# Six heads' masks in one transfer of 128 rows, and three pairs' k transposed on TensorE

## The chip, the core and the metric

One NeuronCore of a Trainium2 chip runs the whole kernel. The metric is the device time of one execution in microseconds (us), less is better; the median of several runs is compared. The profiles show one execution each.

## What is computed

Three stages follow each other. The change touches the first one only.

```python
q, k, v: (2, 8, 768, 64) float32;  lam: (8,), 0.97 to 0.99
# attention with decay, in blocks of 64 positions
Dmask = where(i >= j, lam[h] ** (i - j), 0)
out   = (q @ k.T * Dmask) @ v + (q * lam[h] ** (i + 1)) @ kv_state
kv_state = lam[h] ** block * kv_state + (k * lam[h] ** (block - 1 - j)).T @ v
# x = out as (2, 768, 512); then a token mixer and a channel MLP
h  = relu(x^T @ w_tok1) @ w_tok2;     u  = x + h^T
y  = u + relu(u @ w_ch1) @ w_ch2
# then real(fft2(y)), a norm and a second MLP (512 -> 2048 -> 512), each with a residual
```

## The kernel before, in words

**Tiling of the attention.** The kernel takes blocks of C = 128 positions (NC = 6 a sequence), which gives the same result as blocks of 64. Two heads share the 128 partitions; such a *pair* is the unit. There are NP = 4 pairs for each of 2 batches, numbered 0 to 7 (pairs 4 to 7 are the second batch). Positions within a block are stored in reverse for k, v and kT, so that a mask entry depends on the sum of row and column.

**What a pair loads.** `load_kp` reads k with head dimensions on the partitions (kT, 384 KB) into one of four places `kps` of the tile `kp`; place i serves pairs i and i + 4. `load_qkv` reads q (same layout), and k and v with positions on the partitions, into a tile `qkv_b_hp` of three used quarters of 384 KB each; its last quarter takes `qs`, q times the powers of lam. k thus comes from memory twice, in two layouts.

**What a pair computes.** `attention_scores` (s): 24 matmuls of kT with q into PSUM; VectorE multiplies them with the masks `dT` (line 420) into `st`; GpSimd makes `qs` (line 424). `attention_states` (u): ScalarE scales k by the decay (line 438, in place), TensorE multiplies it with v into a bank `u_...`, and VectorE runs the chain of states (lines 448 and 450). `attention_out` (r): ScalarE puts the states into block diagonals (line 462), TensorE adds `st` times v and the state times `qs` in banks `po_...`, and ScalarE copies them to `xT` (line 473).

**The masks.** `dT` holds one 128 x 128 mask for each of 8 heads, in the tile `att`. Those of heads 0 and 1 are built on VectorE by doubling (line 374). For the other six, the powers of lam are built in `pw8`, one partition a head (line 341), written to a scratch in memory (line 344), and read back by `skew` (line 350) so that partition p gets the row that starts at p: first heads 2 to 5, then 6 and 7, in pieces of 512 bytes.

**What sets the order.** TensorE and SP, which issues the loads, run in program order as the code writes it; the other engines' order is placed by a scheduler at build time. The string `EARLY` is the program of the first 90 us: `s`, `u`, `r` with a pair's number, `l` loads a pair (4 to 7), `c` and `d` convert token weights (a weight arrives as 64-bit words and takes one copy on ScalarE, two or three shifts on VectorE and a split on ScalarE and GpSimd), `w` is 8 transposes of the identity that only keep TensorE busy, `x`, `h`, `o` are the token mixer. 22 further such transposes (`keep_warm(22)`) stand ahead of it. At most eight loads are under way at once: each issue waits for the landing of the eighth before it. The tile pools are rings: PSUM banks of `acc_bank` (4) serve `u`, `po`, the warm-up and x; `half_tile` (5) holds the pairs' qkv tiles and later x.

Of the kernel before, what the change touches and what calls it, by code (L numbers as in the profile page):

```python
# [11 lines left out]
F32 = mybir.dt.float32  # L12
# [3 lines left out]
AF = mybir.ActivationFunctionType  # L16
# [19 lines left out]

EARLY = """s0 w u0 w s1 r0 u1 s2 u2 l4 r1 s3 u3 c r2 s4 l5 r3 u4 d d d x00 s5 l6 u5 r4 s6 x01 h00 c r5 c h01 l7 u6 s7 u7 r6 o00
r7 m o01 x10 m x11 m h10 m h11 m m o10 o11 k"""
# [24 lines left out]
def body(ctx: ExitStack, tc: tile.TileContext, qkv, kT, lam, w_tok1, w_tok2,  # L63
# [154 lines left out]
    def stage_abs():  # L218

        if at_["abs"] >= at_["load"]:  # L220
            return
        job = jobs[at_["abs"]]
        kind, key = job
        at_["abs"] += 1
        if kind in ("single", "sums"):
            return
        m = raw_p.tile([P, 512], U32, tag="man", name="m_" + "_".join(map(str, key)), bufs=BUFS["man"])[:, :width(key)]
        mans[job] = m
        with tc.issue_after(lag.get("act", on_act["keys", 3])), behind_urgent():
            lo, hi = words(job)  # L230
            nc.scalar.activation(f32(m), f32(hi), AF.Copy, scale=DOWN)
            if key[0] in "ab":
                halves = raws[job].bitcast(U16)[:, :4 * width(key)].rearrange("p (n t) -> p n t", t=4)
                nc.scalar.activation(lo, halves[:, :, 1], AF.Identity, scale=2.0 ** -13, bias=floor_by)
# [88 lines left out]
    def attention_setup():  # L323

        pw8 = temp(2 * C, "pw8")[:H]
        nc.sync.dma_start(pw8[:, C:C + 1], lam.rearrange("(h o) -> h o", o=1))
        lam_bc = sm_p.tile([P, H], F32, name="lam_bc")
        nc.scalar.dma_start(lam_bc, lam.rearrange("(o h) -> o h", o=1).broadcast_to([P, H]))
        kp = big_tile("kp").rearrange("p (i s) -> p i s", i=4)[:, :, :S]
        kps = [kp[:, i, :].rearrange("p (c j) -> p c j", j=C) for i in range(4)]  # L330
        load_kp(0, 0, kps[0])
        t = half_tile([P, 4, S], "qkv_0_0")
        for i in range(3):
            nc.sync.dma_start(t[:, i, :], qkv[0, 0, :, i])
        load_kp(0, 1, kps[1])
        nc.vector.memset(pw8[:, 0:C - 1], 0.0)
        nc.vector.memset(pw8[:, C - 1:C], 1.0)
        n = 1
        while n < C:
            w = min(n, C - n)  # L340
            ts(out=pw8[:, C + n:C + n + w], in0=pw8[:, C:C + w], scalar1=pw8[:, C + n - 1:C + n], scalar2=None,
               op0=ALU.mult)
            n *= 2
        nc.sync.dma_start(scratch, pw8)
        att = big_tile("att")
        dT = att[:, 0:H * C].rearrange("p (h j) -> p h j", h=H)

        def skew(h0, h1):
            src = bass.AP(scratch.tensor, scratch.offset + h0 * 2 * C, [[1, P], [2 * C, h1 - h0], [1, C]])
            nc.sync.dma_start(dT[:, h0:h1, :], src)  # L350

        load_qkv(0, 1)
        skew(2, 6)

# [9 lines left out]
        while n < C:  # L364
# [7 lines left out]
            for h in range(2):  # L372
                src = bands[i % 2][:, h]
                built = stt(out=dT[:, h, :] if 2 * n == C else bands[1 - i % 2][:, h, C // 2:],
                            in0=src[:, C // 2 - n:C // 2 - n + C], scalar=by[:, h:h + 1], in1=src[:, C // 2:],
                            op0=ALU.mult, op1=ALU.add).ins
# [14 lines left out]
        pair[0, 0] = t  # L391
        return dT, pw, kps, [bd[:, i] for i in range(2)], skew

    def load_qkv(b, hp):
        t = half_tile([P, 4, S], f"qkv_{b}_{hp}")
        nc.sync.dma_start(t[:, 0, :], qkv[b, hp, :, 0])
        nc.sync.dma_start(t[:, 1:3, :], qkv[b, hp, :, 1:3])
        pair[b, hp] = t

    def load_kp(b, hp, kp):  # L400
        nc.sync.dma_start(kp, kT[b, hp].rearrange("p (c j) -> p c j", j=C))

    pair = {}

    def attention_scores(b, hp, dT, pw, kp):
# [5 lines left out]
        for g, cs in enumerate((range(4), range(4, NC))):  # L411
# [6 lines left out]
            for a in range(2):  # L418
                st = st2[:, a] if g else temp(4 * C, f"st_{n}_{a}").rearrange("p (c j) -> p c j", c=4)
                tt(out=st, in0=ps[a][:, :m * C].rearrange("p (c j) -> p c j", c=m),  # L420
                   in1=dT[:, 2 * hp + a:2 * hp + a + 1, :].to_broadcast([P, m, C]), op=ALU.mult)
                for i, c in enumerate(cs):
# [6 lines left out]
    def attention_states(b, hp, dT, pw):  # L429
# [6 lines left out]
        with tc.issue_after(on_act[behind]):  # L436
            for a in range(2):
                on_act["keys", NP * b + hp] = nc.scalar.activation(
                    kn[:, :NC - 1, a * D:(a + 1) * D], kn[:, :NC - 1, a * D:(a + 1) * D], AF.Copy,
                    scale=dT[:, 2 * hp + a, C - 1:C]).ins  # L440
        ups = acc_bank(f"u_{n}")
# [577 lines left out]
    with tc.manual_schedule(engines={ENG.SP, ENG.PE}):  # L1019
        dT, pw, kps, bds, skew = attention_setup()  # L1020

# [4 lines left out]
        load(2)  # L1026
        skew(6, H)
        load(3)
# [5 lines left out]
        def scores(n):  # L1034
            attention_scores(n // NP, n % NP, dT, pw, kps[n % NP])

        def states(n):
# [12 lines left out]
        def constants():  # L1050
# [4 lines left out]
        keep_warm(22)  # L1055
        acts = {"s": scores, "u": states, "r": result, "l": load, "c": convert, "x": token_in, "h": token_hidden,
                "o": token_out, "m": run, "w": lambda: keep_warm(8), "k": constants, "d": lambda: convert(1, load=False)}
# [148 lines left out]
```

## Time and profile before

| | |
|---|---|
| median of 3 runs | 605.16 us (603.69 to 605.57) |
| the profiled execution | 605.05 us, of which its span 603.1 |
| TensorE busy (PE) | 585.0 us, 97% of the span |
| VectorE busy (DVE) | 410.4 us, 68% |
| ScalarE (ACT), GpSimd (POOL) | 269.9 us, 45%; 138.8 us, 23% |
| granted clock of TensorE | 1.000 (full speed) over the span |
| bytes moved by DMA | 65.58 MB, mean 109 GB/s |

Busy shares are means over stages of very different kind; the attention takes the first 70 us or so, in which the token mixer already begins. A group of instructions is named by its line; `out<-in` are the program's tiles. "[x <-E]" behind a row is idle time ahead of it and what ended it.

### The profile page before, as it was taken

To read this page: it belongs to the slowest core of one execution; us is meant where nothing else is said; L and a number is where in the kernel's file an instruction comes from. 1 tells how busy PE (TensorE), PEld (TensorE's weight loads), DVE (VectorE), ACT (ScalarE), POOL (GpSimd) and SP (SyncE) were. 2 spreads that over 40 slices of the span, in tenths; PEclk is the share of its full clock that TensorE was granted. 3 is DMA by queue.
4 is the path that set the end of the run, shared out by engine and by line. 5 is a ranking of instruction groups with operands and counts; after the bars stand their busy time and mean duration, and the time that the engine had idled before them with its cause. 6 is when DMAs were issued, how large, how long until landed. Compare 5 with 4: busy or idle time off the path is not lost. (4 is left out here: it accounts for less than half of the span.)

```text
span 603.1 us, 9588 instructions
## 1 busy us (share of the span) xinstructions
PE 585.0 (97%) x3704; PEld 545.9 (91%) x3704; DVE 410.4 (68%) x768; ACT 269.9 (45%) x536; POOL 138.8 (23%) x119
## 2 busy tenths in 40 slices
PE   8789999999999999999999999999999999999997
PEld 7777899999999999999989899899899888999886
DVE  6788893474586656848796896768775765664435
ACT  2756981255475555534454451324533434431110
POOL 5252331023230041101364110013501213120000
PEclk9999999999999999999999999999999999999999
DMA  7964431014448767410232000002521232200005
GB/s 275 407 261 158 185 122 60 0 71 141 137 148 265 245 192 219 146 64 2 57 101 71 19 2 35 18 1 58 168 88 36 88 122 88 87 2 1 0 1 209
DMA packets 24637, 65.58 MB, mean 109 GB/s; under 512 B 2824, under 2 KB 3984, under 8 KB 24592
## 3 DMA queue, kind: packets, MB, share of 16 engines
q1 hardware_dynamic: 24304, 64.83, 32.1%
q8 instruction: 29, 0.48, 0.3%
q10 hardware_dynamic: 288, 0.14, 0.1%
q14 instruction: 16, 0.13, 0.1%
HBM read 54.99 MB, written 9.97 MB: 108 GB/s over the span
## 5 line engine op out<-in xcount | busy, mean ns | idle before, releaser
L526 DVE SCALAR_TENSOR_TENSOR hid<-ph,hid 128x384 fp32r<-128x384 f32 x68 | 37.6, 553 | 59.6 <-ACT hid L525 59.4
L145 PE MATMUL ac<-w_b,hid 128*128 128x512 f32 x192 | 75.8, 395 | 0.0
L144 PE MATMUL ac<-w_b,hid 128*128 128x512 f32 x192 | 75.7, 394 | 0.0
L143 PE MATMUL ac<-w_b,hid 128*128 128x512 f32 x192 | 74.9, 390 | 0.0
L143 PE MATMUL ph<-uh,w_a 128*128 128x384 f32 x192 | 64.7, 337 | 0.0
L143 PE MATMUL ac<-hid,w_b 128*128 128x384 f32 x192 | 64.5, 336 | 0.0
L144 PE MATMUL ac<-hid,w_b 128*128 128x384 f32 x192 | 64.3, 335 | 0.0
L145 PE MATMUL ph<-uh,w_a 128*128 128x384 f32 x192 | 64.2, 335 | 0.0
L145 PE MATMUL ac<-hid,w_b 128*128 128x384 f32 x192 | 64.2, 334 | 0.0
L144 PE MATMUL ph<-uh,w_a 128*128 128x384 f32 x192 | 64.2, 334 | 0.0
L525 ACT ACTIVATE hid<-ph 128x384 fp32r<-128x384 f32 x68 | 33.1, 487 | 69.3 <-PE ph L145 68.9
L287 POOL TENSOR_TENSOR w_a<-m_a,w_a 128x512 fp32r<-128x512 f32 x18 | 25.5, 1418 | 131.9 <-ACT w_a L286 131.9
L145 PEld LDWEIGHTS ac<-w_b,hid 128*128 128x128 f32 x192 | 36.0, 188 | 7.7
L144 PEld LDWEIGHTS ac<-w_b,hid 128*128 128x128 f32 x192 | 36.0, 188 | 6.1
L143 PEld LDWEIGHTS ac<-w_b,hid 128*128 128x128 f32 x192 | 36.1, 188 | 5.8
L287 POOL TENSOR_TENSOR w_b<-m_b,w_b 128x512 fp32r<-128x512 f32 x18 | 25.3, 1403 | 49.6 <-ACT w_b L286 32.4
L143 PEld LDWEIGHTS ph<-uh,w_a 128*128 128x128 f32 x192 | 36.1, 188 | 0.4 <-issue 0.2
L144 PEld LDWEIGHTS ac<-hid,w_b 128*128 128x128 f32 x192 | 36.1, 188 | 0.3 <-DVE hid L526 0.3
L144 PEld LDWEIGHTS ph<-uh,w_a 128*128 128x128 f32 x192 | 36.1, 188 | 0.1
L143 PEld LDWEIGHTS ac<-hid,w_b 128*128 128x128 f32 x192 | 36.1, 188 | 0.0
L145 PEld LDWEIGHTS ph<-uh,w_a 128*128 128x128 f32 x192 | 36.0, 188 | 0.0
L145 PEld LDWEIGHTS ac<-hid,w_b 128*128 128x128 f32 x192 | 36.0, 188 | 0.0
(504 smaller groups left out, 1467.0 us busy)
## 6 DMA issues: line engine op xcount, KB each, us to landing
qkv<-qkv SPq DMA_DIRECT2D x7, 768.0 KB, 10.0
single_scratch<-m_a SPq DMA_DIRECT2D x16, 256.0 KB, 4.4
qkv<-qkv SPq DMA_DIRECT2D x10, 384.0 KB, 5.9
kp<-kT SPq DMA_DIRECT2D x8, 384.0 KB, 6.9
out<-u SPq DMA_DIRECT2D x11, 256.0 KB, 2.1
single_scratch<-m_b SPq DMA_DIRECT2D x10, 256.0 KB, 5.3
raw_t_0d<-w_tok SPq DMA_DIRECT2D x2, 384.0 KB, 9.3
raw_t_1d<-w_tok SPq DMA_DIRECT2D x2, 384.0 KB, 2.9
```

The costliest lines, as they stand in the source:

```text
L143: nc.tensor.matmul(ps, wt[0], xt[0], start=first, stop=False, **kw)
L144: nc.tensor.matmul(ps, wt[0], xt[1], start=False, stop=False, **kw)
L145: nc.tensor.matmul(ps, wt[1], xt[0], start=False, stop=last, **kw)
L287: nc.gpsimd.tensor_tensor(out=t[:, 1, :n], in0=src, in1=f32(t[:, 0, :n]), op=ALU.subtract)
L525: mark("act", nc.scalar.activation(hi, ps, AF.Relu))
L526: mark("dve", stt(out=lo, in0=ps, scalar=0.0, in1=f32(hi), op0=ALU.max, op1=ALU.subtract))
```

## The change

The six far heads' powers are now built on one partition with the head as the inner index, so that the scratch holds x0h0, x0h1, ... One transfer (`far_masks`) fills `att` for all six: partition p reads 768 consecutive values (3 KB) that start at 6p. A head's mask is then a view of that tile in which neighbours lie six values apart (`far[:, :, h]`); heads 0 and 1 stay packed. The powers' place is that of pairs 2 and 3 in `kp`, which isn't loaded any more.

For pairs 1, 2 and 3 kT isn't read. The new `attention_turn` (word `t`) has TensorE transpose k's six blocks into two banks `pk` of the `acc_bank` ring, before k is scaled in place, and ScalarE copies them to `kps`. Loads of these pairs come one quarter at a time, k first. `t3` stands ahead of `u2`; one conversion `d` stands ahead of `u4`. Pairs 4 to 7 load kT as before.

```diff
--- before.py
+++ after.py
@@ -34,7 +34,10 @@
 BIG = 12 * NQ
 
 
-EARLY = """s0 w u0 w s1 r0 u1 s2 u2 l4 r1 s3 u3 c r2 s4 l5 r3 u4 d d d x00 s5 l6 u5 r4 s6 x01 h00 c r5 c h01 l7 u6 s7 u7 r6 o00
+TURNED = (1, 2, 3)
+
+
+EARLY = """s0 w u0 t1 w s1 r0 t2 u1 s2 t3 u2 l4 r1 s3 u3 c r2 s4 l5 r3 d u4 d d x00 s5 l6 u5 r4 s6 x01 h00 c r5 c h01 l7 u6 s7 u7 r6 o00
 r7 m o01 x10 m x11 m h10 m h11 m m o10 o11 k"""
@@ -226,7 +229,7 @@
             return
         m = raw_p.tile([P, 512], U32, tag="man", name="m_" + "_".join(map(str, key)), bufs=BUFS["man"])[:, :width(key)]
         mans[job] = m
-        with tc.issue_after(lag.get("act", on_act["keys", 3])), behind_urgent():
+        with tc.issue_after(lag.get("act", on_act[("keys", 3) if key == ("t1", 0) else ("out", 2)])), behind_urgent():
             lo, hi = words(job)
             nc.scalar.activation(f32(m), f32(hi), AF.Copy, scale=DOWN)
             if key[0] in "ab":
@@ -322,35 +325,38 @@
 
     def attention_setup():
 
-        pw8 = temp(2 * C, "pw8")[:H]
-        nc.sync.dma_start(pw8[:, C:C + 1], lam.rearrange("(h o) -> h o", o=1))
+        kp = big_tile("kp").rearrange("p (i s) -> p i s", i=4)[:, :, :S]
+        kps = [kp[:, i, :].rearrange("p (c j) -> p c j", j=C) for i in range(4)]
+
+
+        n_far = H - 2
+        powers = kp[0:1, 2:4, :].rearrange("o i s -> o (i s)").rearrange("o (x h) -> o x h", h=n_far)
+        nc.sync.dma_start(powers[:, C:C + 1, :], lam[2:H].rearrange("(o x h) -> o x h", o=1, x=1))
         lam_bc = sm_p.tile([P, H], F32, name="lam_bc")
         nc.scalar.dma_start(lam_bc, lam.rearrange("(o h) -> o h", o=1).broadcast_to([P, H]))
-        kp = big_tile("kp").rearrange("p (i s) -> p i s", i=4)[:, :, :S]
-        kps = [kp[:, i, :].rearrange("p (c j) -> p c j", j=C) for i in range(4)]
         load_kp(0, 0, kps[0])
         t = half_tile([P, 4, S], "qkv_0_0")
-        for i in range(3):
-            nc.sync.dma_start(t[:, i, :], qkv[0, 0, :, i])
-        load_kp(0, 1, kps[1])
-        nc.vector.memset(pw8[:, 0:C - 1], 0.0)
-        nc.vector.memset(pw8[:, C - 1:C], 1.0)
+        nc.sync.dma_start(t[:, 0, :], qkv[0, 0, :, 0])
+        nc.vector.memset(powers[:, 0:C - 1, :], 0.0)
+        nc.vector.memset(powers[:, C - 1:C, :], 1.0)
         n = 1
         while n < C:
             w = min(n, C - n)
-            ts(out=pw8[:, C + n:C + n + w], in0=pw8[:, C:C + w], scalar1=pw8[:, C + n - 1:C + n], scalar2=None,
-               op0=ALU.mult)
+            tt(out=powers[:, C + n:C + n + w, :], in0=powers[:, C:C + w, :],
+               in1=powers[:, C + n - 1:C + n, :].to_broadcast([1, w, n_far]), op=ALU.mult)
             n *= 2
-        nc.sync.dma_start(scratch, pw8)
+        nc.sync.dma_start(scratch.rearrange("(o n) -> o n", o=1), powers.rearrange("o x h -> o (x h)"))
+        for i in range(1, 3):
+            nc.sync.dma_start(t[:, i, :], qkv[0, 0, :, i])
         att = big_tile("att")
-        dT = att[:, 0:H * C].rearrange("p (h j) -> p h j", h=H)
-
-        def skew(h0, h1):
-            src = bass.AP(scratch.tensor, scratch.offset + h0 * 2 * C, [[1, P], [2 * C, h1 - h0], [1, C]])
-            nc.sync.dma_start(dT[:, h0:h1, :], src)
-
-        load_qkv(0, 1)
-        skew(2, 6)
+        far = att[:, 2 * C:H * C].rearrange("p (j h) -> p j h", h=n_far)
+        dT = [att[:, h * C:(h + 1) * C] for h in range(2)] + [far[:, :, h] for h in range(n_far)]
+
+        def far_masks():
+            nc.sync.dma_start(att[:, 2 * C:H * C], bass.AP(scratch.tensor, scratch.offset, [[n_far, P], [1, n_far * C]]))
+
+        load_kp(0, 1, kps[1])
+        load_qkv(0, 1, far_masks)
 
         bands = [temp(2 * (C // 2 + C), f"band_{i}").rearrange("p (h j) -> p h j", h=2) for i in range(2)]
         for t_ in bands:
...
@@ -389,16 +395,32 @@
                                     in1=pw[:, :, n - 1:n].to_broadcast([P, NP, n]), op=ALU.mult)
             n *= 2
         pair[0, 0] = t
-        return dT, pw, kps, [bd[:, i] for i in range(2)], skew
-
-    def load_qkv(b, hp):
+        return dT, pw, kps, [bd[:, i] for i in range(2)]
+
+    def load_qkv(b, hp, first=lambda: None):
         t = half_tile([P, 4, S], f"qkv_{b}_{hp}")
-        nc.sync.dma_start(t[:, 0, :], qkv[b, hp, :, 0])
-        nc.sync.dma_start(t[:, 1:3, :], qkv[b, hp, :, 1:3])
+        if NP * b + hp in TURNED:
+            nc.sync.dma_start(t[:, 1, :], qkv[b, hp, :, 1])
+            first()
+            for i in (2, 0):
+                nc.sync.dma_start(t[:, i, :], qkv[b, hp, :, i])
+        else:
+            nc.sync.dma_start(t[:, 0, :], qkv[b, hp, :, 0])
+            nc.sync.dma_start(t[:, 1:3, :], qkv[b, hp, :, 1:3])
         pair[b, hp] = t
 
     def load_kp(b, hp, kp):
-        nc.sync.dma_start(kp, kT[b, hp].rearrange("p (c j) -> p c j", j=C))
+        if NP * b + hp not in TURNED:
+            nc.sync.dma_start(kp, kT[b, hp].rearrange("p (c j) -> p c j", j=C))
+
+    def attention_turn(b, hp, kp):
+        kn = pair[b, hp][:, 1, :].rearrange("p (c j) -> p c j", j=C)
+        for g, cs in enumerate((slice(0, 4), slice(4, NC))):
+            m = len(range(NC)[cs])
+            pk = acc_bank(f"pk_{b}_{hp}_{g}")
+            for i in range(m):
+                nc.tensor.transpose(pk[:, i * C:(i + 1) * C], kn[:, cs.start + i, :], ident)
+            nc.scalar.activation(kp[:, cs, :], pk[:, :m * C].rearrange("p (c j) -> p c j", c=m), AF.Copy)
 
     pair = {}
 
@@ -418,7 +440,7 @@
             for a in range(2):
                 st = st2[:, a] if g else temp(4 * C, f"st_{n}_{a}").rearrange("p (c j) -> p c j", c=4)
                 tt(out=st, in0=ps[a][:, :m * C].rearrange("p (c j) -> p c j", c=m),
-                   in1=dT[:, 2 * hp + a:2 * hp + a + 1, :].to_broadcast([P, m, C]), op=ALU.mult)
+                   in1=dT[2 * hp + a].rearrange("p (o j) -> p o j", o=1).to_broadcast([P, m, C]), op=ALU.mult)
                 for i, c in enumerate(cs):
                     sts[c, a] = st[:, i, :]
         nc.gpsimd.tensor_tensor(
...
@@ -1017,14 +1039,13 @@
             step["i"] += 1
 
     with tc.manual_schedule(engines={ENG.SP, ENG.PE}):
-        dT, pw, kps, bds, skew = attention_setup()
+        dT, pw, kps, bds = attention_setup()
 
         def load(n):
             load_kp(n // NP, n % NP, kps[n % NP])
             load_qkv(n // NP, n % NP)
 
         load(2)
-        skew(6, H)
         load(3)
         for _ in range(3):
             load_next()
@@ -1034,6 +1055,9 @@
         def scores(n):
             attention_scores(n // NP, n % NP, dT, pw, kps[n % NP])
 
+        def turn(n):
+            attention_turn(n // NP, n % NP, kps[n % NP])
+
         def states(n):
             attention_states(n // NP, n % NP, dT, pw)
 
@@ -1053,7 +1077,7 @@
         keep_warm(22)
-        acts = {"s": scores, "u": states, "r": result, "l": load, "c": convert, "x": token_in, "h": token_hidden,
+        acts = {"s": scores, "t": turn, "u": states, "r": result, "l": load, "c": convert, "x": token_in, "h": token_hidden,
...
-    scratch = nc.dram_tensor("pw_scratch", (H, 2 * C), F32, kind="Internal").ap()
+    scratch = nc.dram_tensor("pw_scratch", ((H - 2) * 2 * C,), F32, kind="Internal").ap()
```

On SP, which issues the loads, the program's start was this (`pw_101` is the tile of the powers, `qkv_1` pair 1):

```order
L326 DMA pw_101<-lam 8x1
L401 DMA kp<-kT 128x768
L334 DMA qkv_0_107<-qkv 128x768 x3
L401 DMA kp<-kT 128x768
L344 DMA pw_scratch<-pw_101 8x256
L396 DMA qkv_1_123<-qkv 128x768
L397 DMA qkv_1_123<-qkv 128x1536
L350 DMA att<-pw_scratch 128x4x128
```

and it is now this, in which the powers are in `kp`:

```order
L334 DMA kp<-lam 1x6
L414 DMA kp<-kT 128x768
L339 DMA qkv_0_106<-qkv 128x768
L348 DMA pw_scratch<-kp 1x1536
L350 DMA qkv_0_106<-qkv 128x768 x2
L403 DMA qkv_1_121<-qkv 128x768
L356 DMA att<-pw_scratch 128x768
L406 DMA qkv_1_121<-qkv 128x768 x2
```

The scratch write moved ahead of pair 0's k and v, the masks ahead of pair 1's v and q, and there is one transfer of masks where there were two.

On ScalarE, from pair 1's scaled k (L438) to pair 3's, before:

```order
L438 ACTIVATE qkv_1_123<-qkv_1_123,att 128x5x64 x2
L473 ACTIVATE xT_179<-po_0_0_291 128x384
L473 ACTIVATE xT_179<-po_0_1_303 128x384
L438 ACTIVATE qkv_2_165<-qkv_2_165,att 128x5x64 x2
L462 ACTIVATE att<-state_1_330 64x2x64 x2
L462 ACTIVATE att<-state_1_330 64x3x64 x2
L462 ACTIVATE att<-state_2_373 64x2x64 x2
L473 ACTIVATE xT_179<-po_1_0_387 128x384
L462 ACTIVATE att<-state_2_373 64x3x64 x2
L473 ACTIVATE xT_179<-po_1_1_399 128x384
L438 ACTIVATE qkv_3_170<-qkv_3_170,att 128x5x64 x2
```

and now, with the line numbers of the changed program (L460 for L438, L484 for L462, L495 for L473):

```order
L460 ACTIVATE qkv_1_121<-qkv_1_121,att 128x5x64 x2
L495 ACTIVATE xT_177<-po_0_0_299 128x384
L495 ACTIVATE xT_177<-po_0_1_311 128x384
L423 ACTIVATE kp<-pk_2_0_325 128x512
L423 ACTIVATE kp<-pk_2_1_331 128x256
L460 ACTIVATE qkv_2_163<-qkv_2_163,att 128x5x64 x2
L484 ACTIVATE att<-state_1_348 64x2x64 x2
L484 ACTIVATE att<-state_1_348 64x3x64 x2
L423 ACTIVATE kp<-pk_3_0_378 128x512
L423 ACTIVATE kp<-pk_3_1_384 128x256
L484 ACTIVATE att<-state_2_401 64x2x64 x2
L495 ACTIVATE xT_177<-po_1_0_415 128x384
```

Pair 2's copies of `pk` moved in ahead of its scaled k, pair 3's ahead of the block diagonals of pair 2.

On GpSimd, near the start, `ident` is what the warm-up transposes read; before:

```order
masks.py:197 MEMSET ident 128x128
masks.py:199 ISA
masks.py:199 AFFINE_SELECT ident<-ident 128x128
L361 MEMSET att 128x1280
L371 TENSOR_TENSOR lp<-lam_bc 128x2
```

and now:

```order
masks.py:197 MEMSET ident 128x128
L367 MEMSET att 128x1280
masks.py:199 ISA
masks.py:199 AFFINE_SELECT ident<-ident 128x128
L377 TENSOR_TENSOR lp<-lam_bc 128x2
```

The clearing of `att` moved ahead of the second operation on `ident`.

## Rows read from the trace of the kernel before

**Rows 1.** Windows of the span: busy us of each engine, granted clock, DMA share, GB/s.
```profile
core 0: us, PE busy (x) PEld busy (x) DVE busy (x) ACT busy (x) POOL busy (x), PEclk, DMA share, GB/s
4.00:11.00 7.00, 6.61 (x77) 5.88 (x77) 6.32 (x24) 1.01 (x2) 3.45 (x14) 1.00 1.03 415
11.00:15.00 4.00, 3.81 (x68) 3.45 (x64) 1.01 (x4) 1.34 (x4) 2.98 (x2) 1.00 0.85 262
15.00:38.00 23.00, 18.41 (x310) 16.60 (x312) 18.07 (x41) 15.85 (x37) 9.51 (x6) 1.00 1.02 406
38.00:60.00 22.00, 20.17 (x216) 16.12 (x212) 18.95 (x38) 13.54 (x32) 7.15 (x6) 1.00 0.42 136
```

**Rows 2.** Timeline of TensorE, 0 to 45 us: start, us, work, [idle before].
```profile
12.19 0.66 PE L468 MATMUL po<-st,qkv 128*64 128x128 f32 x8
...
15.95 1.25 PE L444 MATMUL u<-qkv 128*64 128x64 f32 x20 [1.13 <-ACT qkv L438]
17.50 1.61 PE L417 MATMUL s<-qkv,kp 64*128 64x128 f32 x24 [0.31 <-DVE state L448]
19.98 1.19 PE L444 MATMUL u<-qkv 128*64 128x64 f32 x19 [0.87 <-ACT qkv L438]
...
23.56 1.61 PE L417 MATMUL s<-qkv,kp 64*128 64x128 f32 x24
25.10 1.08 PE L444 MATMUL u<-qkv 128*64 128x64 f32 x19
29.46 1.61 PE L417 MATMUL s<-qkv,kp 64*128 64x128 f32 x24 [0.83 <-DVE m_t L257]
...
36.61 0.66 PE L488 MATMUL px<-ident,xT 128*128 128x128 f32 x4 [1.38 <-ACT xT L473]
...
43.52 1.75 PE L417 MATMUL s<-qkv,kp 64*128 64x128 f32 x17 [0.86 <-DVE st L420]
```

**Rows 3.** Timeline of VectorE, 0 to 45 us and 60 to 72 us.
```profile
2.16 1.76 DVE L341 TENSOR_SCALAR pw<-pw 8x1 f32<-8x1 f32 x7 [0.83 <-DMA pw<-lam]
...
15.34 1.95 DVE L420 TENSOR_TENSOR st<-s,att 128x512 f32<-128x512 f32 x4 [3.23 <-DMA att<-pw_scratch]
...
24.75 1.95 DVE L420 TENSOR_TENSOR st<-s,att 128x512 f32<-128x512 f32 x4 [2.00 <-PE s L417]
...
31.84 1.94 DVE L420 TENSOR_TENSOR st<-s,att 128x512 f32<-128x512 f32 x4
...
42.78 1.94 DVE L420 TENSOR_TENSOR st<-s,att 128x512 f32<-128x512 f32 x4
...
65.10 0.69 DVE L254 SCALAR_TENSOR_TENSOR m_b<-m_b,raw_b_0d 128x512 uint32<-128x512 uint32 x1 [1.07 <-issue]
```

**Rows 4.** Timeline of SP, which issues the loads, 0 to 45 us.
```profile
9.09 0.38 SPq L350 DMA_DIRECT2D att<-pw_scratch  x1
```

**Rows 5.** DMA issues of the page: KB each, median us from issue to landing.
```profile
raw_t_1d<-w_tok SPq DMA_DIRECT2D x2, 384.0 KB, 2.9
```

**Rows 6.** Timeline of GpSimd, 0 to 45 us.
```profile
1.25 1.17 POOL L361 MEMSET att<- 128x1280 f32 x1
...
29.40 1.97 POOL L424 TENSOR_TENSOR qkv<-qkv,att 128x640 f32<-128x640 f32 x1 [6.12 <-DMA qkv<-qkv]
```

**Rows 7.** Groups of ScalarE by line and form: busy us, mean ns of one.
```profile
L286 ACT ACTIVATE w_b<-m_b 128x512 fp32r<-128x512 f32 x18 | 11.4, 633 | 11.0 <-DVE m_b L259 11.0
...
L779 ACT ACTIVATE gr<-xT 128x512 f32<-128x512 f32 x4 | 4.5, 1152 | 0.0
```

**Rows 8.** Line 910 from 288 to 300 us: weight loads, ns min/median/max.
```profile
L910 PEld LDWEIGHTS pu<-ident,xT x8: 211/225/239, 291.1 to 294.5; 128*128 128x128 f32 x8
L910 PEld LDWEIGHTS pu<-ident,gr x8: 139/140/165, 291.6 to 295.0; 128*128 128x128 f32 x8
```

**Rows 9.** Groups of VectorE by line and form: the masking.
```profile
L420 DVE TENSOR_TENSOR st<-s,att 128x512 f32<-128x512 f32 x16 | 10.3, 682 | 5.3 <-DMA att<-pw_scratch 3.2 <-PE s L417 2.0
...
L420 DVE TENSOR_TENSOR st<-s,att 128x256 f32<-128x256 f32 x16 | 5.9, 412 | 0.0
```

More of the change, by code (lines that the diff above doesn't have):

```diff
@@ L373, in attention_setup @@
                 src = bands[i % 2][:, h]
-                built = stt(out=dT[:, h, :] if 2 * n == C else bands[1 - i % 2][:, h, C // 2:],
+                built = stt(out=dT[h] if 2 * n == C else bands[1 - i % 2][:, h, C // 2:],
                             in0=src[:, C // 2 - n:C // 2 - n + C], scalar=by[:, h:h + 1], in1=src[:, C // 2:],
@@ L439, in attention_states @@
                     kn[:, :NC - 1, a * D:(a + 1) * D], kn[:, :NC - 1, a * D:(a + 1) * D], AF.Copy,
-                    scale=dT[:, 2 * hp + a, C - 1:C]).ins
+                    scale=dT[2 * hp + a][:, C - 1:C]).ins
         ups = acc_bank(f"u_{n}")
```

## The prediction

> **What bounds the kernel now.** The windows come first [rows 1]. Between 15 and 38 us the DMA engines move 406 GB/s with a busy share of 1.02: the queue never runs dry, while TensorE is busy for 18.4 of 23 us. That stretch waits for q, k, v and kT. From 38 to 60 us DMA is at 0.42, and VectorE (18.95 of 22) and TensorE (20.2) are the full ones. After that TensorE has hardly a gap (the page's 97%), so whatever the first 60 us gain or lose reaches the end undiminished. One more window stands out: 415 GB/s from 4 to 11 us, but 262 from 11 to 15. There the mask transfers run, in rows of 512 bytes.
>
> The waits of TensorE say where [rows 2]: 1.13 us ahead of the second pair's `u`, 0.83 ahead of the fifth pair's scores at 29.46, 0.86 ahead of the seventh's at 43.52. On VectorE [rows 3] the second pair's masking stands for 3.23 us until the masks land, at 15.34. SP issues that load only at 9.09 [rows 4], once the powers have landed in the scratch behind five loads of 384 KB.
>
> **The change, part by part.**
>
> *Bytes.* Three kT loads go: 1.18 MB, at 406 GB/s 2.9 us. One mask load in rows of 3 KB replaces two of 512 bytes; in the slow window 4 us moved 262 where 415 was possible, which is 1.4 to 1.5 us to win. So the loads behind the masks land 3 to 4.3 us earlier.
>
> *The start.* The powers are now built by seven two-input operations on one partition, up to 384 wide, instead of up to 64. The old chain took 1.76 us [rows 3]; at some 1.05 ns an element (from the masking rows below, 682 less 412 ns for 256 elements) the wider steps add about 0.5. From 2.16 that ends at 4.4; the scratch write is issued then, and k and v of pair 0, which went out early before, stand behind it: k0 at 4.7. A load of this size that finds the queue empty lands 2.9 us after its issue [rows 5], so k0 is there at 7.6 and each next load one transfer (0.96 us) later. GpSimd now clears `att` (1.17 us, [rows 6]) ahead of the identity's second operation, so the warm-up transposes on it begin up to 1.2 us later, and the first scores with them. All this is covered by what is late next: q1, the sixth load from k0 on (k0, v0, k1, masks, v1, q1), five times 0.96 behind it: **12.4 us**. Pair 1's scores now begin there, and their masking 1.2 later, once the first bank is full (pair 3's scores of 23.56 were masked from 24.75, [rows 2, 3]), at 13.6 instead of 15.34, since the masks (land near 10.5) are no longer last. VectorE is **1.8 us ahead** here. The bound from above is a mask load as slow as before (2.4 us, not 1): q1 at 13.9, 0.3 ahead.
>
> *Transposes.* Four transposes took 0.66 us from the first start to the last end [rows 2]; of that some 0.15 is the last one's drain, which the next work covers, so six are 0.8 and the 18 are 2.3 us of TensorE. The first six lie in the wait for q1. But r0 (2.6 us, from 12.19 to the gap ahead of 15.95, [rows 2]) filled the wait for the masks before, and now it stands behind pair 1's scores: scores 12.4 to 14.0, r0 to 16.7, t2 and u1 to 18.3. Pair 2's scores then begin at 18.3 (17.50 before, [rows 2]): 0.8 late in spite of the earlier start. From there to the fifth pair's scores the old order took 11.96 us, 1.7 of it waiting (0.87 for ScalarE's scaled k ahead of 19.98, 0.83 at the end). With both waits gone, as k2 and q4 land well ahead, and t3's 0.8 in place, TensorE alone would begin s4 near 29.0, against 29.46.
>
> *Evictions.* Six copies of pk, at most the 633 ns of a copy of 512 columns [rows 7] and near 0.4 us for 256, are 3 us of ScalarE. They stand ahead of the scaled k of the same round. ScalarE was busy 15.85 of 23 us [rows 1], and its long waits there (for masks, for k2) are the ones that go, so I count these at nothing except where the next part makes them late.
>
> *The layout of the masks.* This costs most. In one row of 3 KB the six heads' values lie interleaved, so each masking operation of pairs 1 to 3, in both batches, reads its mask 24 bytes apart; before, 4 bytes. No row of VectorE shows such a read, so I bound it. Below: nothing, if the other input sets the pace. Above: ScalarE's gather of every sixth value takes 1152 ns for 512 where a plain copy takes 633 [rows 7], that is 1.02 ns an element. Between: TensorE's weight load of every sixth column takes 225 ns where the same load from packed data takes 140 [rows 8], 1.76 ns a column. Two engines that both slow down when they read SBUF so make a third likely. I take the level of the weight load, 1.76 ns an element: VectorE has 1.05 now, so +0.7 ns on 1536 elements (two of 512, two of 256, [rows 9]): **+1.1 us for each of six pairs**.
>
> The Trainium skill, SBUF — State Buffer, section "Door 1: The DMA port swizzle", says that SBUF is read in lines of 16 bytes, that at least two hits a line are needed for full speed, and that four fp32 is as far as one can step for free. It makes no exception for an engine, so by it rival A below is out and the sum lies somewhere from the forecast up to B; it names no size. Rows 7 and 8 agree with it, but no row of VectorE does or doesn't, and so A keeps a chance.
>
> *What 1.1 us a pair does.* VectorE masks pair 1 from 13.6 to 16.6, pair 2 from 19.6 to 22.7, and its state chain ends 1.4 us later than before. ScalarE's row after it (block diagonals, xT, then k3's scaling) moves along, so u3 begins at 26.2 instead of 25.10 [rows 2], r2 ends at 29.5, and s4 begins at 29.5: **even** with 29.46. The fifth pair's masks are of heads 0 and 1, packed and fast: masking at 32.0 (31.84 before). Next comes the conversion of the token weights, which in the old run was stretched behind GpSimd's product (1.97 us from 29.40, [rows 6], and its successors) because that product started when q4 and q5 landed. With these earlier, VectorE's two shifts end 0.3 earlier, px_2 comes at 36.3 instead of 36.61, and the sixth pair's masking at 41.4 instead of 42.78 (the third weight's shift no longer collides with GpSimd's product of the seventh pair): **1.4 ahead**. Then two slow pairs in the stretch that VectorE bounds: 1.1 for the sixth pair (0.3 ahead), 1.1 for the seventh (0.8 behind, of which 0.6 is a gap of VectorE that x's eviction no longer opens): h00's last inputs are **0.2 late**. The eighth pair's 1.1 meets a wait of VectorE of 1.07 us ahead of 65.10 [rows 3], but only part of the masking lies ahead of it; I count 0.4.
>
> Sum: 0.2 + 0.4 = **+0.6 us** on the profiled 605.05, so 605.65; that execution is 0.1 from the median of 605.16. Forecast **605.6**.
>
> **Rivals.**
>
> *A, the strided masks cost nothing on VectorE.* For it: the operation reads its other input from PSUM and already takes 1.05 ns an element, which may hide the second stream. Against: ScalarE and TensorE. Then u3 isn't late, s4 comes at 29.0, px_2 at 35.1 (w_t_1's conversion 1.4 earlier), the sixth pair's masking at 40.1 and the seventh's scores 2.1 us before 43.52. Nothing behind is anchored to a clock: -2.1, **603.0**.
>
> *B, they cost what ScalarE pays.* +1.02 ns on 1536 elements is 1.56 us a pair. u3 is 0.5 later than in the forecast, s4 30.0, px_2 36.8; two pairs in the stretch that VectorE bounds put h00 1.4 behind, the eighth adds 0.8: +2.2, **607.2**. It passes the mark of slower (0.3%, 1.8 us, about what a measurement of this kernel can tell from no change) from some 1.4 us a pair on.
>
> *C, the start doesn't get faster.* If the mask load stays slow or the scratch write lands late, q1 comes at 13.9 and TensorE, which has no wait left to give before s4, carries 1.5 us: s4 near 30.5, some 0.7 of it absorbed by VectorE's stretch: +1.4 on the forecast, **607**. For it: DMA was slow just where this scratch was read. Against: 128 rows of the size of every other load here.
>
> *D, fewer bytes change nothing, with masks as fast as before*: DMA is earlier, yet 2.3 us of transposes and r0's new place take all of it: **605**.
>
> **How the numbers follow.** Forecast 0.45 (604.4 to 606.8), A 0.27 (602 to 604), B 0.15, C 0.08, D 0.05. Of A two thirds lie beyond 0.3% faster, and a little of the forecast: faster 0.25. Of B and C 0.8, and a little of the forecast: slower 0.24. Same: 0.51. The range leaves out the outer third of A and of B: 602.5 to 607.6.
>
> **What would show it.** In the new profile: DMA at 400 GB/s without the dip at 11 to 15 us; the second pair's masking at 13.6 (right) or after 15 (C); and first of all the masking operation at 512 columns: 0.68 us (A), 1.04 (forecast), 1.2 (B), with the same line for pairs 0 and 4 at 0.68. u3 near 26.2, s4 near 29.5, the sixth pair's masking near 41.4. What would make me wrong otherwise: a wait on a PSUM bank that pk takes from u and po, or a clock that falls in the longer wait ahead of q1 (the rows have 1.0 through 1.1 us of waiting, none longer).

## The result, and the profile after

The changed kernel takes **610.79 us** (median of six runs, 609.44 to 612.48) against 605.64 (603.69 to 606.81) of the kernel before: ratio **1.0089**, 95% interval 1.0069 to 1.0109, that is some 5.4 us slower by the ratio. The forecast of 605.6 and its range, up to 607.6, were wrong. The profiled execution took 609.44 us with a span of 607.6 (603.1 before), so its trace shows 4.5 of the 5.4 us.

The windows of the changed kernel, columns as in [rows 1]:

```profile
4.00:11.00 7.00, 7.00 (x73) 6.42 (x72) 6.44 (x24) 1.01 (x2) 3.53 (x13) 1.00 1.01 316
11.00:15.00 4.00, 1.25 (x12) 1.01 (x10) 1.12 (x4) 3.10 (x8) 1.54 (x1) 1.00 1.01 371
15.00:38.00 23.00, 21.26 (x368) 19.61 (x369) 18.27 (x37) 14.02 (x33) 9.02 (x6) 1.00 0.91 352
38.00:60.00 22.00, 18.98 (x205) 15.42 (x204) 21.62 (x41) 13.96 (x32) 7.58 (x6) 1.00 0.32 102
```

The dip in GB/s has not gone; it has moved forward. From 4 to 11 us the loads run at 316 GB/s instead of 415, and TensorE, which was busy for 3.81 of the 4 us from 11 to 15, is now busy for 1.25. What it waits for is in its timeline:

```profile
10.50 0.88 PE L422 MATMUL pk<-ident,qkv 128*128 128x128 f32 x6
11.21 1.04 PE L1072 MATMUL warm<-ident 128*128 128x128 f32 x8
15.43 1.61 PE L439 MATMUL s<-qkv,kp 64*128 64x128 f32 x24 [3.18 <-DMA qkv<-qkv]
...
29.33 1.19 PE L466 MATMUL u<-qkv 128*64 128x64 f32 x19 [1.19 <-ACT qkv L460]
...
32.91 1.61 PE L439 MATMUL s<-qkv,kp 64*128 64x128 f32 x24
```

Pair 1's scores begin at 15.43, when q1 lands; before, they began at 10.65. u3 and s4 (25.10 and 29.46 in [rows 2]) come 4.2 and 3.5 us later. The queue of SP shows why: the masks' transfer (line 356) goes out at 6.18, ahead of v1 and q1.

```profile
5.24 0.43 SPq L403 DMA_DIRECT2D qkv<-qkv  x1
6.18 0.33 SPq L356 DMA_DIRECT2D att<-pw_scratch  x1
6.55 0.91 SPq L406 DMA_DIRECT2D qkv<-qkv  x2
```

The DMA view of that moment gives the time from issue to landing in its last column:

```profile
att<-pw_scratch SPq DMA_DIRECT2D x1, 384.0 KB, 7.1
```

So the masks land at 13.3, and q1, two loads behind, by 15.4. k1, ahead of them, was there by 9.9 (issued at 5.24, landed after 4.7): the masks' one load of 384 KB landed 3.4 us behind it, where the prediction counts 0.96 from one load to the next.

VectorE's timeline, the masking of pair 0 (packed masks), of pair 1 and of pair 5 (interleaved masks):

```profile
8.40 1.95 DVE L442 TENSOR_TENSOR st<-s,att 128x512 f32<-128x512 f32 x4
...
16.59 3.12 DVE L442 TENSOR_TENSOR st<-s,att 128x512 f32<-128x512 f32 x4 [4.34 <-PE s L439]
...
44.45 3.08 DVE L442 TENSOR_TENSOR st<-s,att 128x512 f32<-128x512 f32 x4
```

The masking as groups by line and form, columns as in [rows 9]:

```profile
L442 DVE TENSOR_TENSOR st<-s,att 128x512 f32<-128x512 f32 x16 | 15.2, 988 | 5.1 <-PE s L439 5.0
...
L442 DVE TENSOR_TENSOR st<-s,att 128x256 f32<-128x256 f32 x16 | 8.4, 574 | 0.0
```

Four of the 16 in each group are packed, at 682 and 412 ns as before [rows 9]; so the strided ones take (16 x 988 - 4 x 682)/12 = 1090 ns and, likewise, 628. A pair's masking takes 3.12 us instead of 1.95.

Theory L, from here: two causes of about equal size, the late q1 and the dearer masking, and the transposes cost nothing. The rivals named beside it: the masking alone (M), the late q alone (Q), the transposes themselves (T).

### The profile page after: what moved, and what is told of

Read it like the earlier page. It is cut to its first block, busy times and chain, and to the rows that moved or that the text cites. A ratio compares the mean times of both kernels' runs of the same rounds, so it can differ in the third digit from the quotient of the medians.

```text
span 607.6 us, 9635 instructions
## 1 busy us (share of the span) xinstructions
PE 587.2 (97%) x3722; PEld 547.5 (90%) x3722; DVE 417.7 (69%) x768; ACT 272.7 (45%) x542; POOL 139.0 (23%) x119
```

## The experiments

All ratios are to the kernel before, run on the same chip, with 95% intervals. Starts, landings and GB/s are read from one profile of each kernel. Of a long line of a diff only the part that changes is shown.

**Taking away one cause at a time.** Pair 1's q ahead of the masks:

```diff
-            first()
-            for i in (2, 0):
-                nc.sync.dma_start(t[:, i, :], qkv[b, hp, :, i])
+            nc.sync.dma_start(t[:, 0, :], qkv[b, hp, :, 0])
+            first()
+            nc.sync.dma_start(t[:, 2, :], qkv[b, hp, :, 2])
```

> The changed kernel with one move: pair 1's q is issued ahead of the masks' transfer, its v behind it. Theory L (two causes: pair 1's q lands at 15.4 us since it stands behind a mask transfer that takes 3 us, and the masking of six pairs costs 1.17 us more each): the scores of pair 1 start at 10.5 to 11.5 us instead of 15.43, TensorE does the third result of pair 0 in the wait for the masks, pair 1's masking starts when the masks land, at 14 to 15 instead of 16.6, and the time is 608 to 609.3 instead of 610.8. Rival M (the masking alone decides, VectorE being the bound to 60 us): within 0.5 of 610.8. Rival Q (the late q alone decides): 605 to 606.5.

Measured: 606.96 us, 1.0038 (1.0023 to 1.0053), by the ratios 3.1 us less than the changed kernel; a little better than expected, and neither M nor Q. Pair 1's scores and masking in its timeline:

```profile
12.85 1.61 PE L439 MATMUL s<-qkv,kp 64*128 64x128 f32 x24
...
14.08 3.13 DVE L442 TENSOR_TENSOR st<-s,att 128x512 f32<-128x512 f32 x4 [1.24 <-PE s L439]
```

The scores came later than the 10.5 to 11.5 expected. q1, issued at 5.71, landed only after 6.5 us, at 12.2, still ahead of the masks but behind the scratch write; and TensorE itself was busy until 12.85: its first warm-ups wait 2.4 us for the identity (1.36 before), and the transposes stand ahead of the scores.

The masks read packed:

```diff
-[far[:, :, h] for h in range(n_far)]
+[att[:, h * C:(h + 1) * C] for h in range(2, H)]
```

> The changed kernel, whose masking and key scales read 128 adjacent numbers of the masks' tile for each head instead of every sixth one (the numbers read are not that head's mask, so the masking is wrong; transfer, order and sizes are as in the changed kernel). Theory L: a pair's masking falls from 3.12 to 1.95 us for pairs 1, 2, 3, 5, 6 and 7, pair 1's scores stay at 15.4, and the time is 607.5 to 609, a part of the six times 1.17 us. Rival M (the masking alone decides): 605 to 606, at or near the kernel before. Rival Q (the late q alone): within 0.5 of 610.8, since TensorE runs behind from 15.4 on with or without the dearer masks.

Measured: 607.17 us, 1.0045 (1.0028 to 1.0062), with every 512-column masking back at 681 ns:

```profile
L442 DVE TENSOR_TENSOR st<-s,att 128x512 f32<-128x512 f32 x16 | 10.3, 681 | 6.2 <-PE s L439 6.2
```

Pair 1's scores stay at 15.23. As theory L has it.

**The two halves of the change, and neither cause.** Transposes with the masks of before (not shown: the powers are again built on eight partitions, and scratch and masks have their old layout):

```diff
-        load_qkv(0, 1, far_masks)
+        load_qkv(0, 1, lambda: skew(2, 6))
...
         load(2)
+        skew(6, H)
```

> Half of the change: three pairs' k transposed by TensorE and not read twice, with the loads' order of the changed kernel (masks of four heads between pair 1's k and v), but the masks as before, one head behind the other, 512-byte rows, four heads in one transfer and two in a later one. Theory L (late q and dearer masking are the two causes, and the turns themselves cost nothing): masking 1.95 us for every pair, pair 1's scores at 14 to 15.5, 606 to 607.5, about as with packed reading in the changed kernel. Rival T (the transposes and their copies are themselves what costs): 608 or more. Rival G (the turns gain what the bytes promise): 603 to 604.5.

Measured: 607.37 us, 1.0028 (1.0010 to 1.0046); pair 1's scores at 14.59 after 2.30 us of waiting for q1. L, not G; T's 608 lies within the interval, and the run with both causes gone settles it.

The interleaved masks without transposes, with the order of the steps of before (that of `EARLY` is not shown):

```diff
-TURNED = (1, 2, 3)
+TURNED = ()
...
-        load_qkv(0, 1, far_masks)
+        load_qkv(0, 1)
+        far_masks()
```

> The other half: the six heads' masks as one transfer of 128 interleaved rows with its strided masking, but every k read twice as before, no transposes, the order of the steps and of pair 1's loads as before (q, then k and v, then the masks). Theory L: q is ahead of the masks, so pair 1's scores start at 10.5 to 11.5, masking waits for the masks to 13.5 to 14.5 (15.34 before) and then costs 1.17 us more for each of six pairs, of which the three at 15 to 30 us are partly made up by the earlier start: 606 to 608. Rival N (the strided masking is hidden, no loss): 604.5 to 605.5.

Measured: 607.83 us, 1.0041 (1.0025 to 1.0056). The time is as expected, but not the start: pair 1's scores began at 12.04, and the masks landed at 15.4, so they gained nothing on the 15.34 of before, and the price of the layout shows.

The transposes, packed masks in two transfers, and q1 ahead of them (the first diff and the third together):

> Both causes taken away: the turns with the masks as before (packed, two transfers), and pair 1's q ahead of the masks. Theory L: scores of pair 1 at 11 to 12.8, masking at 13.5 to 14.5 for 1.95 us, the rest up to 1.5 us earlier than in the kernel before: 602.5 to 604.5. Rival T (transposes, copies and six fewer microseconds of slack on ScalarE cost by themselves): 605.5 or more.

Measured: **603.96 us, 0.9977 (0.9961 to 0.9993)**, faster than both kernels. Its timeline has pair 1's scores and masking at:

```profile
11.74 1.61 PE L438 MATMUL s<-qkv,kp 64*128 64x128 f32 x24
...
13.00 1.95 DVE L441 TENSOR_TENSOR st<-s,att 128x512 f32<-128x512 f32 x4 [0.88 <-PE s L438]
```

The runs make a table of four, in thousandths over the kernel before: q1 late and masks strided +8.9, q1 early +3.8, masks packed +2.8 (+4.5 with the one transfer kept), both -2.3. Moving q1 is worth 5.1 in either row; packing 6.1 in either column (4.4 with the one transfer). Each number is uncertain by about 2, so that the causes add so exactly is luck. The packed kernel of +2.8 and the one of -2.3 also have the old two transfers back, and their warm-ups start at 1.36 again. With both causes gone the kernel is faster than before; what the transposes cost by themselves no run shows.

The clock is in these medians. Of the executions whose mean granted clock was 0.999 or more, the medians are 609.5 us for the changed kernel (two of six), 607.2 with q1 early (seven of twelve), 604.9 with packed masks (two of twelve) and 603.4 with both (six of twelve). There moving q1 is worth 2.2 and 1.5 us, packing 4.6 and 3.8. So at full clock the dearer masking is the larger cause, and much of what the late q1 costs came with a lower clock. The groups are small and from different chips (the kernel before, likewise, had 605.2 and 605.6 on two of them), and with q1 early the five executions at a lower clock were no slower (606.8); so this is a sign and no proof.

**What makes the masks' transfer slow.** Its source as 128 rows of k that do not overlap, then as rows of k that overlap as the scratch's do:

```diff
-bass.AP(scratch.tensor, scratch.offset, [[n_far, P], [1, n_far * C]])
+kT[0, 1]
```

```diff
-bass.AP(scratch.tensor, scratch.offset, [[n_far, P], [1, n_far * C]])
+bass.AP(kT.tensor, kT.offset, [[n_far, P], [1, n_far * C]])
```

> The changed kernel, whose masks' transfer takes 128 rows of 3 KB that lie one behind the other in k (so the masks are not masks; size, queue, target and the strided reading are kept, the wait for the scratch write falls away). Theory L with a slow transfer because its rows overlap, 24 bytes apart in 6 KB: the stretch from 9 to 12 us moves 400 GB/s instead of 169 to 292, pair 1's q lands at 12 to 12.7, its scores start there, and the time is 608 to 609.3. If the target's rows or the many queues were the cause, the transfer stays slow and q lands at 15.

> The changed kernel, whose masks' transfer takes 128 rows of 3 KB that overlap, 24 bytes apart, as in the changed kernel, but from the first 6 KB of k instead of the scratch (so the masks are not masks, and no transfer waits for the scratch write). Theory L (overlapping rows are slow): 9 to 12 us stays under 300 GB/s, pair 1's q lands at 14.5 to 15.5, time 610 to 611. Rival W (the scratch just written is what is slow, or the wait for it): as with rows that do not overlap, q at 12 to 12.7 and 608 to 609.3.

Measured: 607.95, 1.0055 (1.0037 to 1.0072), pair 1's scores at 14.13; and 609.20, 1.0072 (1.0055 to 1.0088), scores at 15.21. Windows of the two, rows apart first:

```profile
8.00:12.00 4.00, 4.00 (x59) 3.64 (x56) 3.29 (x12) 1.51 (x4) 3.10 (x8) 1.00 0.95 320
```

```profile
8.00:12.00 4.00, 2.56 (x36) 2.25 (x37) 3.22 (x12) 0.94 (x3) 3.10 (x8) 1.00 0.94 248
```

Overlap costs (248 against 320 GB/s, scores 1.1 us later), wherever the bytes lie; W falls. The two times alone would not tell, since their intervals overlap. But rows apart were expected at 400 GB/s and at 12 to 12.7. Something else is slow too. Three runs take it apart: neither scratch write nor masks' transfer (both lines of the diff); the write alone (its second line); a plain transfer alone (its first line, and the transfer from `kT[0, 1]`). All read packed masks.

```diff
-        nc.sync.dma_start(scratch.rearrange("(o n) -> o n", o=1), powers.rearrange("o x h -> o (x h)"))
-            nc.sync.dma_start(att[:, 2 * C:H * C], bass.AP(scratch.tensor, scratch.offset, [[n_far, P], [1, n_far * C]]))
```

> The changed kernel without the scratch write and without the masks' transfer; all far pairs are masked with the near pair's masks, read packed (so their masks are wrong). It shows what the start does with no mask transfer at all. If the masks' transfer and the wait behind the scratch write are the whole slowness, the loads run at 400 to 415 GB/s from 4 to 15 us, pair 1's q lands at 10.6 to 11.2 and the time is 601 to 603. If a stretch between 8 and 12 us still moves under 350 GB/s, something else at the start slows the loads.

> As the kernel without masks' transfer, but with the scratch write of 6 KB from one partition put back where it stands, ahead of pair 0's k and v; nothing reads it (all far pairs are masked with the near pair's masks, so wrongly). If the write itself holds the queue up: 330 to 360 GB/s from 4 to 8 us instead of 409, the rest at full speed, pair 1's q 0.6 to 1 us later than without it, time 603 to 604. If the write is free and only the transfer that reads the masks is slow: 400 GB/s from 4 to 15 us and 602.5.

> The changed kernel with the masks' transfer of 128 plain rows of k in place of the masks, no scratch write, and packed reading (so the masks are not masks). It differs from the kernel without masks' transfer by one plain load of 384 KB ahead of pair 1's v and q. If only overlapping rows and the scratch write are slow: 400 GB/s throughout from 4 to 15 us, q one load (0.96 us) later than without the transfer, pair 1's scores at 12.4 to 13.2, 602.5 to 604. If a transfer into the masks' tile is slow by its target: a stretch under 340 GB/s between 8 and 12 us.

Measured: 602.54, 0.9949 (0.9930 to 0.9968); 603.66, 0.9981 (0.9967 to 0.9994); 602.93, 0.9964 (0.9952 to 0.9975). Windows in that order:

```profile
4.00:8.00 4.00, 4.00 (x26) 3.67 (x26) 4.00 (x18) 0.21 (x1) 1.36 (x6) 1.00 1.02 409
8.00:12.00 4.00, 4.00 (x58) 3.64 (x57) 3.25 (x11) 1.43 (x4) 3.09 (x8) 1.00 1.03 407
```

```profile
4.00:8.00 4.00, 4.00 (x22) 3.67 (x22) 4.00 (x18) 0.22 (x1) 1.37 (x6) 1.00 0.97 353
8.00:12.00 4.00, 4.00 (x60) 3.64 (x59) 3.03 (x11) 1.21 (x3) 3.10 (x8) 1.00 0.99 350
```

```profile
4.00:8.00 4.00, 4.00 (x40) 3.83 (x38) 4.00 (x18) 0.22 (x1) 1.37 (x6) 1.00 1.03 409
8.00:12.00 4.00, 3.65 (x46) 3.06 (x44) 3.20 (x12) 2.17 (x6) 3.10 (x8) 1.00 1.03 406
```

A plain load into the masks' tile is as fast as any other. The write of 6 KB alone takes the loads from 409 to 353 and from 407 to 350 GB/s. In the first window that goes with pair 0's k and v, which are issued only behind it, at 4.38 (2.00 without it): the version below that has the write behind them moves 407 GB/s there. In the second the reason is shown by no run here.

The starts of pair 1's scores share out the delay: 12.34 with plain rows and no write, 14.13 with plain rows and the write, 15.21 with overlapping rows of k and the write, 15.43 in the changed kernel. So of 3.1 us some 1.8 come with the write and 1.1 with the overlap; the write is the larger part.

The write put behind pair 0's k and v, in the version with both causes gone:

```diff
-        nc.sync.dma_start(t[:, 0, :], qkv[0, 0, :, 0])
+        for i in range(3):
+            nc.sync.dma_start(t[:, i, :], qkv[0, 0, :, i])
...
-        for i in range(1, 3):
-            nc.sync.dma_start(t[:, i, :], qkv[0, 0, :, i])
```

> The version with the turns, packed masks and pair 1's q ahead of the masks, and the scratch write put behind pair 0's k and v on the queue, where the kernel before has it. If the write holds up what is behind it, pair 0's k and v land up to 0.9 us earlier and pair 1's k and q as well: 603 to 604, up to 0.8 under the version before it (603.96 against 605.74 of the kernel before, 0.9977). Rival: the write only moves the gap to behind pair 0's v, or the masks land later by as much and the masking of pair 1 with them: 604 to 605.

Measured: 603.79, 0.9986 (0.9974 to 0.9999), no difference from 0.9977. The first half of the rival holds: 407 GB/s from 4 to 8 us, and then 277 from 8 to 12, so the gap only moved. Its second half does not: pair 1's masking began at 12.47, earlier than the 13.00 above, and TensorE waits 0.74 us for k3 at 19.25 instead.

**The spread.** The six times of the changed kernel lie at 609.4 to 609.8 and at 611.8 to 612.5. The upper three have a mean granted clock of 0.996 or 0.997; of the lower three two have 1.000, but the third 0.997, so the clock alone does not sort them. One profile, that of the overlapping rows of k, caught the clock falling. Windows (the column ahead of the DMA share is the granted clock), and the scores that began there:

```profile
14.00:15.00 1.00, 0.00 (x0) 0.00 (x0) 0.00 (x0) 0.97 (x3) 0.00 (x0) 1.00 1.05 424
15.00:16.00 1.00, 0.79 (x10) 0.82 (x12) 0.00 (x0) 0.06 (x1) 0.86 (x1) 0.77 1.02 409
16.00:17.00 1.00, 1.00 (x13) 1.00 (x13) 0.02 (x1) 0.00 (x0) 0.67 (x1) 0.50 1.06 423
17.00:18.00 1.00, 1.00 (x11) 0.78 (x10) 1.00 (x2) 0.00 (x0) 0.00 (x0) 0.50 1.02 387
```

```profile
15.21 2.65 PE L439 MATMUL s<-qkv,kp 64*128 64x128 f32 x24 [2.29 <-DMA qkv<-qkv]
```

After waits of 1.44 and 2.29 us TensorE runs at half speed, 1.2 of 2.4 GHz, from 15 to 19 us, and the scores take 2.65 us instead of 1.61. So the changed kernel was run with the wait filled:

```diff
-EARLY = """s0 w u0 t1 w s1 r0
+EARLY = """s0 w u0 t1 w w w w s1 r0
```

> The changed kernel with 24 more warm-up matmuls between pair 1's transposes and its scores, which fill TensorE's wait for q (12.3 to 15.4 us); they write a bank that nobody reads. Theory K (part of the executions are 2 to 3 us longer because the granted clock falls in that wait, as one profile showed with 0.93 for 15 to 38 us and scores of 2.65 us instead of 1.61): the upper group of times at 611.8 to 612.5 goes away, all of them lie at 609 to 610.3, median 609.6. Rival: the spread has another cause, the median stays at 610.8 and the times still reach 612.

Measured: 608.93 us, 1.0062 (1.0049 to 1.0074); all six times, 607.82 to 609.27, lie below all six of the changed kernel, though the kernel before was 0.6 us faster beside them too. The upper group is gone, as theory K has it, and five of the six clocks are at 0.999 or more. Six executions of each are few for a proof. Its profile, 607.2 us, shows the same fall at another place: u7 waits 1.86 us for ScalarE's scaling, and from 68 to 71 us the clock is at 0.50. First TensorE's timeline, then the windows:

```profile
66.64 1.19 PE L466 MATMUL u<-qkv 128*64 128x64 f32 x19 [1.86 <-ACT qkv L460]
```

```profile
68.00:69.00 1.00, 1.00 (x12) 1.00 (x10) 1.00 (x2) 0.99 (x2) 0.00 (x0) 0.50 0.07 29
69.00:70.00 1.00, 1.00 (x12) 1.00 (x11) 0.70 (x2) 0.95 (x4) 0.00 (x0) 0.50 0.02 8
```

## Why the prediction was wrong, point by point

Starts in us, read from the timelines of TensorE:

| | before | forecast | after | q1 early | packed | both |
|---|---|---|---|---|---|---|
| pair 1's scores | 10.65 | 12.4 | 15.43 | 12.85 | 15.23 | 11.74 |
| third px of x00 | 36.61 | 36.3 | 39.57 | 37.35 | 38.50 | 35.89 |
| h00 | 47.01 | 47.2 | 49.82 | 47.59 | 47.59 | 44.98 |
| u7 | 62.66 | | 66.50 | 64.01 | 62.83 | 60.01 |
| span | 603.1 | 603.7 | 607.6 | 604.7 | 603.4 | 601.4 |

(The forecast's span is 603.1 and its sum of 0.6. "Packed" is the changed kernel with its masks read packed, "both" the transposes with the old masks and q1 early.)

**The step that failed is the start**: "q1, the sixth load from k0 on ... 12.4 us". The first half of it was right: the scratch write went out at 4.09 (4.4 forecast), k0 landed at 7.8 (7.6) and k1 at 9.9 (9.5). The masks then landed 3.4 us behind k1, not 0.96, and everything behind them, q1 too, was 3 us late. I had read the old dip of 262 GB/s as the price of 512-byte rows, and had counted the scratch write only as a delay of the issues behind it. The runs show both to be wrong: 3-KB rows are slow as well if they overlap (1.1 us), and the write slows the loads for several us more (1.8 us). The bound from above, 2.4 us and q1 at 13.9, came from the same reading and so was too low. Rival C, at 0.08, had the slow mask load, not the write, and that bound; its +1.4 does not follow from its own terms either (1.5 less 0.7 is 0.8).

**What it does** then moved as a block: u3, s4, the third px and pair 5's masking came at 29.33, 32.91, 39.57 and 44.45, that is 3.1, 3.4, 3.3 and 3.1 us behind the forecast's 26.2, 29.5, 36.3 and 41.4; h00 is 2.6 behind. VectorE's stretch gave back 0.4 of it, not the 0.7 that C counted on. (The prediction's own terms for TensorE alone, 18.3 + 11.96 - 1.7 + 0.8, give 29.4 for s4 and not its 29.0; the forecast took s4 from u3 and r2.)

**The layout of the masks** was priced closely: 1.17 us a pair against 1.1, 1090 ns for 512 columns against 1040, by +0.80 ns an element against +0.7. The level was borrowed from TensorE's weight load, which nothing tied to VectorE, so that it came so close is in part luck. Rivals A and B are out. By the rule of the Trainium skill that the prediction weighed there (SBUF — State Buffer, section "Door 1: The DMA port swizzle") A was out from the start, and the measured row agrees.

**Behind h00** the forecast had 0.4, for the eighth pair's masking. The changed kernel loses another 1.7 us there to the kernel before (2.8 late at h00, 4.5 at the end), while with packed reading it loses nothing more (0.6 and 0.3). But it isn't that masking, which begins only behind u7, and u7 is already 1.0 later than h00 was. u7 waits 1.68 us, against 0.79 before, for ScalarE's scaling of k7 behind the copy of `w_a`, which waits for a split of `m_a` on VectorE. That split takes 1.91 us, since it now begins while GpSimd's product of pair 7 runs; before, it began ahead of the product and took 0.69. Before, then after:

```profile
59.59 0.69 DVE L259 SCALAR_TENSOR_TENSOR m_a<-raw_a_0d,m_a 128x512 uint32<-128x512 uint32 x1
60.35 1.55 POOL L424 TENSOR_TENSOR qkv<-qkv,att 128x640 f32<-128x640 f32 x1 [2.06 <-DMA qkv<-qkv]
```

```profile
62.39 1.91 POOL L446 TENSOR_TENSOR qkv<-qkv,att 128x640 f32<-128x640 f32 x1 [0.74 <-DMA qkv<-qkv]
62.94 1.91 DVE L262 SCALAR_TENSOR_TENSOR m_a<-raw_a_0d,m_a 128x512 uint32<-128x512 uint32 x1
64.88 0.63 ACT L289 ACTIVATE w_a<-m_a 128x512 fp32r<-128x512 f32 x1 [2.76 <-DVE m_a L262]
66.50 1.19 PE L466 MATMUL u<-qkv 128*64 128x64 f32 x19 [1.68 <-ACT qkv L460]
67.71 1.10 DVE L442 TENSOR_TENSOR st<-s,att 128x512 f32<-128x512 f32 x1
```

In every other profile the split begins ahead of the product and takes 0.69, save in that of the filled wait, where the two begin together and it takes 2.07. So this loss is one of place: with either cause alone, and also with rows of k in place of the masks, which have both, it isn't there. The other 0.7 lies behind u7, where the rest takes 541.1 us against 540.4; over the profiles with packed masks it takes 540.2 to 541.4, so no price of the eighth pair can be told there. Sorted so, 605.65 + 2.6 + 1.3 (1.7 less the 0.4 counted) = 609.55 against the profiled execution's 609.44; that is the trace's own difference in the forecast's terms, and no second proof.

**Transposes and evictions**: 0.88 us for six against 0.8, copies of 0.87 us a pair against 1.0. No wait of TensorE in the first 72 us ended with one of these copies, as counted.

**The warm-ups**, put down as covered, were covered only by q1's lateness; with q1 early (landed at 12.2) they are part of what sets 12.85.

**The clock** stood among what would make me wrong. To it I put the rest, from 609.44 to the median of 610.79: supported for one wait by filling it, and only argued for the share of it in each run. The prediction's "none longer" than 1.1 us was misread: its rows also have a wait of 1.38 us, at a granted clock of 1.00.

## What to carry to other kernels

Price a transfer by a row with its own pattern of addresses: 3-KB rows were slow here because they overlap, and a small write ahead of the loads cost more than that. What is issued behind a doubtful transfer takes over its risk, so the load that the next work needs goes ahead of it. Before a layout is chosen for one transfer, count how often an engine reads it afterwards; here one saved issue cost 1.17 us at each of six readings. A wait that is new for TensorE is priced with the clock in mind, since what follows it may run at half speed.

## What the runs showed of the hardware

- With a load of 384 KB into SBUF whose 128 rows overlap, 24 bytes apart, the loads ran at 248 GB/s from 8 to 12 us, against 320 with rows apart beside the same small write and 406 without the write; the work behind it began at 15.21 us, against 14.13 and 12.34.
- A DRAM write of 6 KB from one partition lowered the loads from 407 to 350 GB/s in the 4 us from 8 on, well after it had been issued (4.09); why is open.
- VectorE, with one input from PSUM and one in SBUF with a step of 24 bytes, took 1090 ns for 512 fp32 columns, packed 682.
- The granted clock fell to half after waits of 1.44 and 2.29 us close together, and after one of 1.86 in another run; it stayed at 1.00 through one of 3.18 us in the profile of the changed kernel.
- One VectorE operation on 512 uint32 columns took 0.69 us where it began ahead of a GpSimd product, and 1.91 and 2.07 us in the two profiles where it began behind it or with it.
